# A planned attention and gated-convolution kernel: transfers paced by the megabyte, dummy products bounded by free banks, TensorE's order written out

## The chip, the cores and the metric

The kernel runs on one core of one Trainium2 chip. The metric is the time of one launch on the device, in microseconds (us). Five engines work side by side, each through its own instruction list in order: TensorE (PE, matrix products into PSUM), VectorE (DVE), ScalarE (ACT), GpSimd (POOL) and SyncE (SP), which here issues most of the transfers between HBM and SBUF. Engines meet at semaphores only.

## The reference

Batch 8, 8 heads, 576 positions, 64 elements per head. For every batch and head there are two attentions, and their sum `x` goes through a gated convolution:

```python
q_d, k_d, v_d = means of q, k, v over 4 neighbouring positions      # 144 positions
out_up = repeat(softmax(q_d k_d^T / 8) v_d, 4)                      # coarse attention
mask   = |i - j| < 4
out_local = softmax(where(mask, q k^T / 8, -1e9)) v                 # local attention
x    = (out_up + out_local) as [8, 576, 512]
gate = sigmoid(sum over k<5 of conv_w[k] * x shifted by 4-k positions)
out  = (gate * (x @ w_val)) @ w_out                                 # 512x512 weights
```

## The kernel before

**Work.** The attention runs in 16 steps `i`; a step takes four heads (two tiles `p` of 128 partitions, 32 tiles in all). On TensorE a step is `sla`, `slb` (local scores, two halves, L722), `sd` (coarse scores, L811), `odp` (coarse attention times v, L932), `xa`, `xb` (local probabilities times v, two halves, L888). `odp`, `xa` and `xb` of a step write one pair of PSUM tiles `x`; VectorE adds the coarse result in `xu` (after `xa`) and `xt` (after `xb`), both L903, and so makes a tile of `x` in SBUF.

The projections run over 10 blocks `j` of columns, 8 of 504 and 2 of 288. In a block, `v` is the product with w_val and `o` the product with w_out. Each has four output groups `c`, and in a wide block each group is four pieces `d` of three products each (`product`, L1096 to L1098: the operands are split into a high and a low part, and high times high, high times low and low times high are added). A piece is named `v2.3@0` (group 2, piece 3, block 0). Two PSUM banks of tag `v` hold the groups in turn: group `c` can begin when group `c-2` has been read, by `h` (gate times value, VectorE, L1124) for `v` and by `ob` (ScalarE, L1186) for `o`. Three double banks of tag `a` hold the attention tiles in turn.

VectorE further does for each tile the four steps `tap0` to `tap3` of the convolution (L994), for each step the row maxima and sums `mx`, `sub`, `sum`, `norm`, the transposes `turn`, `cturn`, the maxima `cmx0`, and the low parts `xl` (L969), `hlo` (L1144) and `wlo` (L1076, of the weights). The weights arrive as float64; `val` (L1049) is VectorE's integer step of their conversion. `xl`, `hlo`, `wlo` and `norm` may be put on VectorE or on GpSimd.

**What sets the order.** The program holds a planner that plays the kernel through with a table of durations (L159 to L428): every engine takes its ready operation with the earliest due time. Two engines have their own rule. TensorE takes from a list made by `tensor_order` (L473), within a window of 14; the list's head is the string `FIRST`, and from step 2 on it comes from the rates in `PACE` and `TURN`. SyncE takes transfers whose due time is within `HORIZON`, eight under way at most (L391). The instructions are then emitted in the order of the planned starts, and the semaphores follow from the order in which they were emitted: if `xu` is emitted ahead of `xb` of the same step, `xb` waits for it, because both touch the tile `x`; if it is emitted behind, it doesn't.

**Dummy products.** Before an attention group or the first piece of a projection group, the planner may set dummy products of 288 columns (`keep_warm`, L576) into the bank of that group, to keep TensorE active. Their number comes from `keep_busy` (L430), by the time since the last product.

The lines that the change touches in `keep_busy` and in the loop over the engines:

```python
gap = now - recent[-1][1]                                    # L440
begin = recent[-1][1] if recent else now - n * ns            # L446
if free[e] > now or (e == "SP" and len(flying) >= OUTSTANDING):   # L391
```

Of the kernel before, what the change touches and what calls it, by code (L numbers as in the profile page):

```python
# [162 lines left out]
class Planner:  # L163
# [102 lines left out]
    def simulate(self):  # L266
# [16 lines left out]
        head, prev, flying = 0, None, []  # L283
        code, arrived = 0, [0.0, 0.0]

        def stall(k, begin):
# [184 lines left out]


def tensor_order():  # L473
# [21 lines left out]
    whole = len(chunks) - 2 * 4 * pieces(NFULL) * 2  # L495
    marks = list(PACE) + [(NSTEP, whole - HOLD)]

    def goal(t):
        for (a, m), (b, n) in zip(marks, marks[1:]):
            if t <= b:  # L500
                return int(m + (n - m) * (t - a) / (b - a))

# [821 lines left out]
```

## Time and profile before

| | |
|---|---|
| Three runs | 367.65, 369.12, 465.03 us; median 369.12 |
| The profiled execution | 368.75 us, of which the instructions span 367.0 |
| TensorE, busy | 341.5 us (93%) |
| VectorE, busy | 309.0 us (84%) |
| ScalarE, busy | 208.3 us (57%) |
| GpSimd, busy | 158.2 us (43%) |
| Moved by DMA | 70.95 MB, mean 193 GB/s |

The profile is of one execution. Busy time of an engine is the time in which it had an instruction under way, so an engine that waits for nothing and one that runs slowly at a lowered clock both look busy. TensorE's products overlap their neighbours, so the time from one start to the next is what a product costs. A wait is put down to the engine whose semaphore came last. "Issue" is time in which an engine waited for nothing that the profile shows.

### The profile page before, as it was taken

What the parts mean: (1) busy time and instruction counts of PE and PEld (TensorE: products, weight loads), DVE (VectorE), ACT (ScalarE), POOL (GpSimd) and SP (SyncE); (2) the same over time, 40 slices, a digit from 0 to 9 for tenths busy, and PEclk for the clock granted to TensorE, in tenths of its full rate; (3) what the DMA queues carried; (4) which work ended last, traced back from release to release, by engine and by line L of the source; (5) the groups of instructions that cost most, each with busy time, mean ns of one, the idle gap of its engine ahead of it and who ended that gap; (6) DMA issues with size and microseconds to landing.
All of it is one profiled execution on the core that took longest, in us unless ns stands there. A gap on an engine that the chain in (4) does not pass through costs nothing.

```text
span 367.0 us, 12798 instructions
## 1 busy us (share of the span) xinstructions
PE 341.5 (93%) x5500; PEld 268.2 (73%) x5500; DVE 309.0 (84%) x487; ACT 208.3 (57%) x530; POOL 158.2 (43%) x170
## 2 busy tenths in 40 slices
PE   8669669699999999999999999999799999999996
PEld 5546447577787777777777777777577778788996
DVE  4699989999899999999999998999988993836720
ACT  1388556746676865587555756675376465314421
POOL 6878732955504644434453245633582323001100
PEclk9998889899999999999999999999999999999999
DMA  7999499899897799887989997969523301102012
GB/s 229 352 362 349 113 292 293 226 199 178 272 305 173 234 267 293 234 210 223 293 205 224 274 248 195 220 183 308 140 49 113 116 3 63 51 2 86 28 50 80
DMA packets 23464, 70.95 MB, mean 193 GB/s; under 512 B 3184, under 2 KB 9584, under 8 KB 23408
## 3 DMA queue, kind: packets, MB, share of 16 engines
q1 hardware_dynamic: 17504, 52.39, 41.0%
q0 software_dynamic: 5616, 17.50, 26.5%
q8 instruction: 43, 0.70, 0.7%
q10 hardware_dynamic: 288, 0.26, 0.2%
q14 instruction: 13, 0.11, 0.1%
HBM read 60.69 MB, written 9.44 MB: 191 GB/s over the span
## 4 chain that ended last, share of the span: by engine, by line
PE 62%; DVE 20%; ACT 7%; DMA 4%; issue 3%; SPq 1%; POOL 1%; ACTq 0%; POOLq 0%; DVEq 0%
PE out L1096 8%; PE val L1096 7%; PE out L1097 7%; PE out L1098 7%; DVE gp L994 7%; PE val L1098 6%; PE val L1097 6%; PE x L888 6%; PE x L932 4%; DMA qk<-in_qk 4%; PE sd L811 4%; PE sl L722 2%; DVE xt L903 2%; ACT pd L855 2%; ACT pt L574 2%
## 5 line engine op out<-in xcount | busy, mean ns | idle before, releaser
L994 DVE SCALAR_TENSOR_TENSOR gp<-xt,cw,gp 128x576 f32<-128x576 f32 x128 | 111.4, 902 | 1.3 <-ACT gp L979 0.6
L1096 PE MATMUL val<-xhs,wh_v 128*128 128x504 f32 (+1 forms) x160 | 64.0, 400 | 0.0
L1098 PE MATMUL val<-xls,wh_v 128*128 128x504 f32 (+1 forms) x160 | 60.3, 377 | 0.3 <-POOL xls L969 0.3
L1097 PE MATMUL val<-xhs,wl_v 128*128 128x504 f32 (+1 forms) x160 | 60.0, 375 | 0.0
L1096 PE MATMUL out<-hhl,wh_o 128*128 128x504 f32 (+1 forms) x144 | 58.6, 407 | 0.5 <-DVE h L1124 0.4
L1098 PE MATMUL out<-hhl,wh_o 128*128 128x504 f32 (+1 forms) x144 | 54.7, 380 | 0.0
L1097 PE MATMUL out<-hhl,wl_o 128*128 128x504 f32 (+1 forms) x144 | 54.6, 379 | 0.0
L1005 ACT ACTIVATE gp<-gp 128x576 f32<-128x576 f32 x32 | 21.9, 685 | 28.1 <-DVE gp L994 27.9
L1186 ACT ACTIVATE ob<-out 128x504 f32<-128x504 f32 (+2 forms) x40 | 21.8, 554 | 27.8 <-PE out L1098 24.0
L888 PEld LDWEIGHTS x<-pt,vw 64*64 64x64 f32 x1536 | 26.4, 138 | 14.6 <-issue 6.4
L903 DVE TENSOR_TENSOR xt<-x,od 128x288 f32<-128x288 f32 x64 | 26.0, 441 | 13.0 <-PE x L888 13.0
L1096 PEld LDWEIGHTS val<-xhs,wh_v 128*128 128x128 f32 x160 | 30.3, 190 | 8.5 <-issue 2.9
L1144 POOL TENSOR_TENSOR hhl<-h,hhl 128x504 fp32r<-128x504 f32 (+2 forms) x24 | 26.8, 1148 | 19.7 <-ACT hhl L574 19.1
L1098 PEld LDWEIGHTS val<-xls,wh_v 128*128 128x128 f32 x160 | 30.4, 190 | 5.9 <-POOL xls L969 0.7
L1096 PEld LDWEIGHTS out<-hhl,wh_o 128*128 128x128 f32 x144 | 27.0, 188 | 9.0 <-issue 3.3
L574 POOL COPY pt<-pt 32x576 f32<-32x576 f32 x23 | 16.9, 733 | 38.6 <-PE x L888 29.7
L1097 PEld LDWEIGHTS val<-xhs,wl_v 128*128 128x128 f32 x160 | 30.4, 190 | 4.1
L888 PE MATMUL x<-pt,vw 64*64 64x48 f32 x1536 | 30.1, 225 | 3.3 <-DVE xt L903 2.4
L606 POOL DMA_DIRECT2D vs<-in_vgr x21 | 20.3, 968 | 29.0 <-DMA vs<-in_vgr 20.8
L855 ACT ACTIVATE pd<-pd,crs 128x144 f32<-128x144 f32 x75 | 24.6, 405 | 12.3 <-DVE crs L849 12.2
L722 PE MATMUL sl<-qk 128*24 128x60 f32 x1536 | 26.8, 215 | 4.7 <-issue 2.0
L831 ACT ACTIVATE pd<-sd,cbi 128x144 f32<-128x144 f32 x80 | 29.9, 386 | 2.1 <-DVE h L1124 1.6
(94 smaller groups left out, 675.8 us busy)
## 6 DMA issues: line engine op xcount, KB each, us to landing
qk<-in_qk SPq DMA_DIRECT2D x64, 291.0 KB, 7.3
vw<-in_vw SPq DMA_DIRECT2D x16, 768.0 KB, 6.0
qs<-in_qkr POOLq DMA_DIRECT2D x18, 576.0 KB, 8.2
out_t<-ob SPq DMA_DIRECT2D x32, 252.0 KB, 4.6
vs<-in_vgr POOLq DMA_DIRECT2D x21, 320.0 KB, 7.5
qs<-in_qkr SPq DMA_DIRECT2D x6, 576.0 KB, 10.5
vs<-in_vgr SPq DMA_DIRECT2D x7, 320.0 KB, 7.2
raw_v<-in_w_val SPq DMA_DIRECT2D x4, 512.0 KB, 8.2
```

The source lines that it names most:

```text
L574: (nc.scalar.copy if eng is nc.scalar else eng.tensor_copy)(out=to, in_=of)
L722: nc.tensor.matmul(out=sc[32 * q : 32 * q + BQ, 2 * KW * g : 2 * KW * (g + 1)].rearrange("p (h k) -> p h k", h=2), lhsT=t[:, 1, 3 + blk : ...
L831: nc.scalar.activation(out=pd[:, g, 0:SD], in_=s["cs"][:, g], func=AF.Exp, scale=1.0 / 128.0, bias=s["bi"][:, g : g + 1], accum_out=s["csm ...
L855: nc.scalar.mul(w[:, g], w[:, g], s["crs"][:, g : g + 1])
L888: nc.tensor.matmul(out=s["x", pr][r, part, 0:HALF].rearrange("p (e g j) -> p e g j", e=2, j=BQ)[:, :, g], lhsT=s["vw"][(LO, HI)[pr], n + h ...
L903: nc.vector.tensor_tensor(out=xt, in0=s["x", pr][:, part, 0:HALF].rearrange("p (e j r) -> p e j r", e=2, r=FAC), in1=od.broadcast_to([P, 2 ...
L994: nc.vector.scalar_tensor_tensor(out=s["gp"], in0=s["xt"][:, k : k + S], scalar=cw[:, c, k : k + 1], in1=s["gp"], op0=ALU.mult, op1=ALU.add,)
L1005: nc.scalar.activation(out=s["gp"], in_=s["gp"], func=AF.Tanh, scale=0.5)
L1096: nc.tensor.matmul(out=o, lhsT=wh[:, d, col], rhs=his[d], start=d == 0, stop=False)
L1097: nc.tensor.matmul(out=o, lhsT=wl[:, d, col], rhs=his[d], start=False, stop=False)
L1098: nc.tensor.matmul(out=o, lhsT=wh[:, d, col], rhs=los[d], start=False, stop=d == NC - 1)
L1144: eng.tensor_tensor(out=t["hl"][:, cs], in0=t["h"][:, cs], in1=t["hh"][:, cs].bitcast(F32), op=ALU.subtract)
```

## The change

Five things change, all of them in the planner and its tables:

1. SyncE's transfers are paced by bytes. Counting back over the transfers that SyncE sent, the one with which 2,000,000 bytes are passed has to have landed. The planner notes it in `pace`, and `emit` adds a semaphore wait on it to the later transfer.
2. Dummy products are planned only in the time in which the bank of their group is free. 30 of them become 20; from `sd@2` on there are none.
3. TensorE's list is written out to its end in `FIRST`; `PACE`, `TURN`, `TURNS` and `HOLD` go.
4. The planner's costs of code loading change: 62 instructions at the start, 0.28 more for each operation, 2700 ns for a block instead of 5500, and on top of it the time that the bytes under way still need.
5. `SHIFT` moves 17 more due times, `HORIZON` goes from 25000 to 29000, and in `EARLY` one weight load moves ahead of one load of q and k.

By these the other engines' orders and shares change too. 14 operations come from GpSimd to VectorE: `norm` of steps 3, 9, 11 and 13, `xl` of tiles 7, 12, 17 and 25, `wlo` of chunks 1, 6 and 7, `hlo0.0@3`, `hlo2.0@5` and the half-width `hlo3.1@3`. Eight leave VectorE: to GpSimd `xl` of tiles 5 and 13, `hlo1.0@5` and four half-width `hlo3`, to ScalarE `cnorm@9`.

```diff
-    "raw4 qk6 raw5 qk7 ql6 ql7 raw6 raw7 vw2 vw3"
+    "raw4 raw5 qk6 qk7 ql6 ql7 raw6 raw7 vw2 vw3"
-HORIZON = 25000
+HORIZON = 29000
+FLIGHT = 2000000
-PACE = ((2, 10), (4, 29), (14, 189))
-HOLD = 6
-TURN = (("sla slb", 1, 3), ("sd", 1, 3), ("odp", 0, 3), ("xa", 0, 3), ("xb", 0, 4))
-    "l0 sd0 l1 sd1 odp0 x0 p2 odp1 p4 l2 p2 x1 sd2 p2"
+    "sla0 slb0 sd0 sla1 slb1 sd1 odp0 xa0 xb0 p2 odp1 p4 sla2 slb2 p2 xa1 xb1 sd2 p3 sla3 slb3 p2 sd3 p2 odp2 p2 xa2 p2 xb2 p2 sla4 p2 slb4 sd4 p3 odp3 xa3 "
...
-CODE, FETCH, BEAR = 256, 5500, 300
+CODE, FETCH, BEAR = 256, 2700, 300
...
+    def backlog(self, t):
+
+        left = sum(max(0.0, x[1]) for l in self.queue.values() for x in l) / 1e3 / self.ALONE["SP"]
+        return max(0.0, left - max(0.0, t - self.now))
...
+        def paced(now):
+
+            kept, left = [], FLIGHT
+            for x in reversed(sent):
+                left -= ops[x]["size"]
+                if left < 0:
+                    if x not in end or end[x] > now:
+                        return False
+                    kept = [x]
+                    break
+            self.behind = kept
+            return True
...
-                if free[e] > now or (e == "SP" and len(flying) >= OUTSTANDING):
+                if free[e] > now or (e == "SP" and (len(flying) >= OUTSTANDING or not paced(now))):
...
-                    begin = self.keep_busy(k, begin)
+                    begin = self.keep_busy(k, begin, banks_free(k, 0))
...
-            gap = now - recent[-1][1]
+            gap = now - max(recent[-1][1], free)
...
-            begin = recent[-1][1] if recent else now - n * ns
+            begin = max(recent[-1][1], free) if recent else now - n * ns
...
-            o["fn"](*([self.engines[self.who[k]]] if o["pick"] else []))
+            self.sent[k] = o["fn"](*([self.engines[self.who[k]]] if o["pick"] else []))
+            for x in self.pace.get(k, ()):
+                self.after(self.sent[k], self.sent[x])
...
+    def after(late, early):
+        tc.add_manual_dep(
+            late.ins,
+            early.ins.name,
+            mybir.DependencyInfo(mybir.DependencyClass.Sync, mybir.DependencyReason.DATA),
+            reason="transfers under way",
+        )
```

**TensorE around the last group of `v` in block 0.** `sl_913` are the scores of step 4, `sl_838` those of step 3; `val_2` and `val_3` are groups 2 and 3 of block 0, and `sd_912` are the coarse scores of step 3; line 579 sets the dummies. In the changed file a line stands 20 further down. Before:

```order
L722 MATMUL sl_913<-qk_78 24x60 x2
L722 MATMUL sl_913<-qk_79 24x60 x2
L579 MATMUL val_3_1000<-const-float32-1.0 128x288 [waits DVE_49]
L579 MATMUL val_3_1000<-const-float32-1.0 128x288 x4
L1096 MATMUL val_3_1000<-xhs,wh_v 128x504
L1097 MATMUL val_3_1000<-xhs,wl_v 128x504
L1098 MATMUL val_3_1000<-xls,wh_v 128x504
```

Now:

```order
L742 MATMUL sl_838<-qk_81 24x60 x2
L1116 MATMUL val_2_805<-xhs,wh_v 128x504
L1117 MATMUL val_2_805<-xhs,wl_v 128x504
L1118 MATMUL val_2_805<-xls,wh_v 128x504
L1116 MATMUL val_3_907<-xhs,wh_v 128x504 [waits DVE_49]
L1117 MATMUL val_3_907<-xhs,wl_v 128x504
L1118 MATMUL val_3_907<-xls,wh_v 128x504
L831 MATMUL sd_912<-qs_708 32x144 x20
```

The five dummies ahead of group 3 are gone, the wait for VectorE (for `h1@0`, which frees the bank) stands at the group's first product. The scores of step 4, which stood ahead of group 3, are further down the list, and the coarse scores of step 3, which stood ahead of group 2, now follow the first piece of group 3.

**VectorE around `h1@0`**, the read that frees that bank (`h_1`). `mx`, `ex<-sl` and `cmx` are row maxima and subtraction of step 3, `hhl` the low part of `h0`. Before:

```order
L1049 SCALAR_TENSOR_TENSOR raw_o_678<-raw_o_678 128x512 [waits DMAHW5_49]
L772 STREAM_TRANSPOSE pt_942<-ex 128x768
L744 TENSOR_REDUCE mx_975<-sl_749 128x24
L861 STREAM_TRANSPOSE pdt_982<-pd 128x800 [waits Activation_49]
L749 TENSOR_TENSOR ex<-sl_749,mx_975 128x24x30 [waits DVE_49]
L821 TENSOR_REDUCE cmx_988<-sd_850 128x5 [waits PE_49]
L1124 SCALAR_TENSOR_TENSOR h_1_992<-gp_593,val_1_637 128x504
L758 TENSOR_REDUCE sm_998<-ex 128x24 [waits Activation_49]
L744 TENSOR_REDUCE mx_1015<-sl_913 128x24 [waits PE_49]
L994 SCALAR_TENSOR_TENSOR gp_747<-xt_84,cw,gp_747 128x576
L994 SCALAR_TENSOR_TENSOR gp_847<-xt_85,cw,gp_847 128x576
L994 SCALAR_TENSOR_TENSOR gp_747<-xt_84,cw,gp_747 128x576 [waits DVE_49]
```

Now:

```order
L792 STREAM_TRANSPOSE pt_823<-ex 128x768 [waits Pool_49]
L881 STREAM_TRANSPOSE pdt_831<-pd 128x800 [waits Activation_49]
L1144 SCALAR_TENSOR_TENSOR h_1_836<-gp_567,val_1_643 128x504 [waits PE_49]
L1014 SCALAR_TENSOR_TENSOR gp_723<-xt_84,cw,gp_723 128x576
L1014 SCALAR_TENSOR_TENSOR gp_730<-xt_85,cw,gp_730 128x576
L1014 SCALAR_TENSOR_TENSOR gp_723<-xt_84,cw,gp_723 128x576 [waits DVE_49]
L764 TENSOR_REDUCE mx_904<-sl_838 128x24 [waits PE_49]
L769 TENSOR_TENSOR ex<-sl_838,mx_904 128x24x30 [waits DVE_49]
L1096 TENSOR_TENSOR wl_o<-raw_o_654,wh_o 128x512 [waits Activation_49]
L1096 TENSOR_TENSOR wl_o<-raw_o_640,wh_o 128x512 [waits Pool_49]
L1014 SCALAR_TENSOR_TENSOR gp_730<-xt_85,cw,gp_730 128x576
L1014 SCALAR_TENSOR_TENSOR gp_723<-xt_84,cw,gp_723 128x576
```

The three operations of step 3 (`mx`, `sub`, `cmx0`) stood ahead of `h1@0` and now stand behind it; two `wl_o` (`wlo@6`, `wlo@7`) have come in behind them from GpSimd.

**SyncE at the loads of w_val.** `DMAHW0` to `DMAHW7` are eight semaphores that SyncE's transfers use in turn. Before:

```order
L1063 DMA raw_v_253<-in_w_val 128x512 [waits DMAHW3_49]
L1063 DMA raw_v_287<-in_w_val 128x512 [waits DMAHW4_49]
L663 DMA vw_291<-in_vw 128x1536 [waits DMAHW5_49]
L601 DMA vs_295<-in_vgr 128x640 [waits DMAHW6_49]
L1063 DMA raw_v_327<-in_w_val 128x512 [waits DMAHW7_49]
L1063 DMA raw_v_331<-in_w_val 128x512 [waits DMAHW0_49]
L658 DMA qk_78<-in_qk 64x1164 [waits DMAHW1_49,DVE_49,PE_49]
L658 DMA qk_78<-in_qk 64x1164 [waits DMAHW2_49]
```

Now:

```order
L1083 DMA raw_v_285<-in_w_val 128x512 [waits DMAHW3_49]
L1083 DMA raw_v_289<-in_w_val 128x512 [waits DMAHW4_49]
L683 DMA vw_293<-in_vw 128x1536 [waits DMAHW5_49]
L621 DMA vs_326<-in_vgr 128x640 [waits DMAHW6_49,DMAHW1_49]
L1083 DMA raw_v_367<-in_w_val 128x512 [waits DMAHW7_49,DMAHW3_49]
L1083 DMA raw_v_377<-in_w_val 128x512 [waits DMAHW4_49,DMAHW0_49]
L678 DMA qk_78<-in_qk 64x1164 [waits DMAHW5_49,DVE_49,PE_49]
L678 DMA qk_78<-in_qk 64x1164 [waits DMAHW2_49]
```

Before, each transfer waits for the one that used its semaphore, eight transfers earlier. Now the third and fourth load of w_val wait for the first and second as well, and some transfers behind them wait later or earlier than by the count of eight.

## Rows read from the trace of the kernel before

**Rows 1.** The head of the profile's page.

```profile
span 367.0 us, 12798 instructions
```

**Rows 2.** Busy time by stretch, us: start and end, length, then each engine (instructions), clock.

```profile
0.00:80.00 80.00, 62.04 (x1197) 45.79 (x1197) 68.66 (x90) 45.54 (x116) 50.68 (x59) 0.91 0.87 268
80.00:280.00 200.00, 195.75 (x3446) 150.67 (x3446) 189.78 (x311) 127.25 (x336) 92.57 (x95) 1.00 0.84 224
```

**Rows 3.** Timeline of TensorE, 58 to 88 us: start, duration, engine, line, operation, idle before.

```profile
58.74 1.43 PE L811 MATMUL sd<-qs 128*32 128x144 f32 x40
...
68.58 4.38 PE L579 MATMUL val<-const-float32-1.0 128*128 128x288 f32 x10 [2.98 <-DVE h L1124]
72.58 0.61 PE L1096 MATMUL val<-xhs,wh_v 128*128 128x504 f32 x1
...
74.96 1.46 PE L932 MATMUL x<-pdt,vs 32*64 32x145 f32 x40
...
77.24 1.61 PE L888 MATMUL x<-pt,vw 64*64 64x48 f32 x96
...
79.16 0.60 PE L1096 MATMUL out<-hhl,wh_o 128*128 128x504 f32 x1
...
85.88 0.34 PE L711 MATMUL sl<-mask_b,ident_b 128*32 128x360 bf16 x4
...
86.67 0.32 PE L711 MATMUL sl<-mask_b,ident_b 128*32 128x360 bf16 x4
```

**Rows 4.** Timeline of VectorE, 44 to 77 us, same columns.

```profile
44.16 1.28 DVE L1076 TENSOR_TENSOR wl_v<-raw_v,wh_v 128x512 fp32r<-128x512 f32 x2
...
52.41 0.91 DVE L821 TENSOR_REDUCE cmx<-sd 128x5 f32<-128x720 f32 x1 [1.38 <-PE sd L811]
...
64.55 0.86 DVE L744 TENSOR_REDUCE mx<-sl 128x24 f32<-128x720 f32 x1
...
66.26 0.86 DVE L749 TENSOR_TENSOR ex<-sl,mx 128x720 f32<-128x720 f32 x1
67.05 0.89 DVE L821 TENSOR_REDUCE cmx<-sd 128x5 f32<-128x720 f32 x1
67.86 0.66 DVE L1124 SCALAR_TENSOR_TENSOR h<-gp,val 128x504 f32<-128x504 f32 x1
...
70.09 6.19 DVE L994 SCALAR_TENSOR_TENSOR gp<-xt,cw,gp 128x576 f32<-128x576 f32 x6
76.21 0.67 DVE L1144 TENSOR_TENSOR hhl<-h,hhl 128x504 fp32r<-128x504 f32 x1
```

**Rows 5.** Costliest groups of VectorE: busy us, mean ns of one.

```profile
L994 DVE SCALAR_TENSOR_TENSOR gp<-xt,cw,gp 128x576 f32<-128x576 f32 x128 | 111.4, 902 | 1.3 <-ACT gp L979 0.6
```

**Rows 6.** TensorE by stretch: length, busy, granted clock, DMA share, GB/s.

```profile
68.50:72.50 4.00, 3.92 (x9) 0.57 0.55 115
72.50:76.00 3.50, 3.50 (x44) 1.00 1.11 203
```

**Rows 7.** Who waited for whom on TensorE, 80 to 367 us: total, times, longest.

```profile
PE x L888 <- DVE xt L903: 2.4, 1, 2.4
```

**Rows 8.** Groups of VectorE that keep shapes apart: busy us, mean ns of one.

```profile
L969 DVE TENSOR_TENSOR xls<-xt,xhs 128x576 fp32r<-128x576 f32 x17 | 13.5, 810 | 2.2 <-ACT xhs L574 1.7 <-POOL xhs L574 0.5
L765 DVE TENSOR_TENSOR ex<-ex,rs 128x720 f32<-128x720 f32 x10 | 10.6, 1058 | 0.0
```

**Rows 9.** Timeline of TensorE: the longest idle time with no releaser shown.

```profile
40.26 0.71 PE L932 MATMUL x<-pdt,vs 32*64 32x145 f32 x11 [3.17 <-issue]
```

**Rows 10.** DMA issues on the page: count, KB each, us from issue to landing.

```profile
qk<-in_qk SPq DMA_DIRECT2D x64, 291.0 KB, 7.3
```

**Rows 11.** Timeline of VectorE: the integer step on the weights, two pairs apart.

```profile
38.17 4.23 DVE L1049 SCALAR_TENSOR_TENSOR raw_v<-raw_v 128x512 uint32<-128x512 uint32 x2
...
61.42 2.32 DVE L1049 SCALAR_TENSOR_TENSOR raw_o<-raw_o 128x512 uint32<-128x512 uint32 x3
```

**Rows 12.** Timeline of GpSimd at the first of those stretches.

```profile
40.16 3.46 POOL L691 TENSOR_TENSOR qs<-qs,qk 128x432 f32<-128x432 f32 x2
```

More of the change, by code (lines that the diff above doesn't have):

```diff
@@ L179, with __init__ @@
     SHARE = 0.5
-    def __init__(self, engines):
-        self.ops = {}
-        self.engines = engines
+    def __init__(self, engines, after):
+        self.ops, self.sent = {}, {}
+        self.engines, self.after = engines, after
     def op(self, key, eng, dur, fn, deps=(), free=(), banks=(), cols=(0, 0), size=0, port=(), code=0):
@@ L282, in simulate @@
         heapq.heapify(wake)
-        head, prev, flying = 0, None, []
-        code, arrived = 0, [0.0, 0.0]
+        head, prev, flying, sent, self.pace = 0, None, [], [], {}
+        code, arrived = 62, [0.0, 0.0]
         def stall(k, begin):
             o = ops[k]
-            n = o["code"] + 4 * self.idle.get(k, 0)
+            n = o["code"] + 4 * self.idle.get(k, 0) + 0.28
             dur, late, new = o["opts"]["PE"], 0.0, []
             have = arrived + new
-            for block in range(code // CODE + 1, (code + n) // CODE + 1):
+            for block in range(int(code // CODE) + 1, int((code + n) // CODE) + 1):
                 t = begin + late + dur * (block * CODE - code) / max(n, 1)
                 late += max(0.0, have[block] - t)
-                new.append(max(t, have[block]) + FETCH)
+                t = max(t, have[block])
+                new.append(t + FETCH + dma.backlog(t))
                 have = arrived + new
@@ L408, in simulate @@
                     arrived += new
-                    code += o["code"] + 4 * self.idle[k]
+                    code += o["code"] + 4 * self.idle[k] + 0.28
                     for tag, rel in o["banks"]:
@@ L420, in simulate @@
                 if o["size"]:
-                    flying += [k] * (e == "SP")
+                    if e == "SP":
+                        flying.append(k)
+                        self.pace[k] = self.behind
+                        sent.append(k)
                     dma.add("POOL" if e == "POOL" else "SP", free[e], o["size"], k)
@@ L428, in simulate, with keep_busy @@
         self.start, self.end, self.who = start, end, who
-    def keep_busy(self, k, now):
+    def keep_busy(self, k, now, free):
         dur = self.ops[k]["opts"]["PE"]
@@ L493, in some @@
         seq.extend((n, s) for n in names.split() if 0 <= s < NSTEP)
[L495 to L501, printed above, removed]
     for word in FIRST.split():
@@ L508, in tensor_order @@
             some({"l": "sla slb", "x": "xa xb"}.get(name, name), i)
-    for s in range(TURNS, NSTEP):
-        seen = 0
-        for names, ahead, n in TURN:
-            seen += n / sum(n for *_, n in TURN)
-            proj(max(0, goal(s + seen) - pos))
-            some(names, s + ahead)
     proj(len(chunks))
@@ L600, in run @@
                 u[nm] = inp.tile(shape, F32, tag=nm, name=f"{nm}{b}", bufs=2)
-                nc.sync.dma_start(out=u[nm], in_=src[b, 0])
+                return nc.sync.dma_start(out=u[nm], in_=src[b, 0])
             return run
@@ L1213, in cw_in @@
     def cw_in():
-        nc.sync.dma_start(out=cw_raw, in_=conv_w)
+        return nc.sync.dma_start(out=cw_raw, in_=conv_w)
     cw_parts = f64_parts(cw_raw)
```

16 lines of the change are left out of this document (8 added, 8 removed), and 4 rows, old and new, of the table FIRST.

## The prediction

> **What bounds the kernel now.** I read the head of the page, then busy time by stretch, then the timeline of the engine that is busiest in each stretch, and last the waits.
>
> By stretch the kernel is two kernels. From 80 to 280 us TensorE is busy 195.75 of 200 us and VectorE 189.78 [rows 2]: TensorE sets the pace, and VectorE has only 200 - 189.78 = 10.2 us to spare. From 0 to 80 us TensorE is busy 62.04 us, much of it with dummies and at a lower clock, while VectorE has 68.66 us of work [rows 2]. So the opening is a chain through VectorE's order, and what TensorE gets out of an edit there counts only as far as VectorE, or work moved behind, lets it. From the first `out` piece at 79.16 us on [rows 3] TensorE works nearly without a hole: after 80 us the one wait of size is 2.4 us of `xb` for `xu` [rows 7]. Whatever brings that first `out` piece forward, less the TensorE work that is put off beyond it, arrives at the end.
>
> **The sum starts** at the profiled execution's own 368.75 us (span 367.0 [rows 1], 1.75 around it). The median of the runs shown, 369.12, is 0.4 above it.
>
> **The dummies ahead of `v3.0@0`.** The bank comes free when `h1@0` ends; then TensorE runs ten dummy records from 68.58 and begins the real piece at 72.58 [rows 3]. All five go: 4.00 us earlier. What they bought is the clock: after 2.98 us of idle [rows 3] the granted clock was 0.57 in those 4.00 us, so mostly 1.2 GHz, and 1.00 after them [rows 6]. Left out, the pieces themselves run through that time: 4.00 x (1 - 0.57) = 1.7 us lost. In the new list the engine has the scores of step 3 and `v2.3` to do just before, so its idle time should be shorter than 2.98. I take half, 0.9, with 0 and 1.7 as ends. The Trainium skill ("TensorE: Matmul & The Clock Gate", section Why this matters for your kernels) says to avoid idle gaps between bursts of products, since the clock drops and the next burst starts slow; this speaks against leaving dummies out, and the clock of 0.57 agrees. By that rule the loss would be the whole 1.7, and on TensorE alone the gain is 0.8 us smaller.
>
> **VectorE ahead of `h1@0`.** It ended at 67.86 + 0.66 = 68.52 [rows 4]. `mx`, `sub` and `cmx0` of step 3 move behind it: 0.86 + 0.86 + 0.89 = 2.61 [rows 4]. One weight part (`wlo@1`) comes in ahead: 1.28 / 2 = 0.64 [rows 4]. So it ends at 66.55. Also `cmx0@2` waited 1.38 us for `sd@2` [rows 4], which itself stood behind two dummies that now go; the operations before it change too, so I take half, 0.7, with 0 and 1.38 as ends. `h1@0` then ends at 65.9, and `v3.0@0` begins there.
>
> **From there to the first `out` piece.** TensorE: four pieces of group 3 (three took 74.96 - 72.58 = 2.38, so 3.17), `sd@3` 1.43, `odp@2` 1.46, `xa` and `xb` 1.61 [rows 3], together 7.67, and 0.9 for the clock: 74.4. VectorE has to reach `hlo0.0@0`: six taps, `mx`, `sub`, two `wlo`, `hlo`. Taps at their mean of 902 ns [rows 5] are 5.41; with 0.86 + 0.86 + 1.28 + 0.67 [rows 4] that is 9.08, so 75.0. With the six taps as slow as they were, 6.19 [rows 4], it is 75.7. VectorE is later than TensorE: 75.4 between its two. That is 79.16 - 75.4 = 3.8 us earlier, and the clock's loss lies under VectorE's lead. Put off beyond it is `sla@4`, `slb@4`, 2 x (86.67 - 85.88) = 1.58 us [rows 3]. **Net 2.2 us.** Ends: no gain at `cmx0`, slow taps (76.4): 1.2; whole gain, taps at their mean (74.3): 3.3. The single dummies ahead of the first two `out` pieces go too; there I count nothing, because the low parts `hlo2` and `hlo3`, now on GpSimd, are what the third and fourth piece will wait for instead.
>
> **After 80 us.** Before, `xb@12` waited 2.4 us for `xu`, which VectorE reached late [rows 7]. In the new list `xb@12` no longer waits for VectorE, since `xu` is emitted behind it: 2.4 us go. But seven other `xb` still do, and `xb@9` stands just one piece behind `xa@9` where there were several. Such a wait is worth between 0 and the 2.4 seen; I take half. **Net 1.2 us.**
>
> **VectorE's load.** 14 operations come, 8 leave. Coming: four `norm` at 1.06, four `xl` at 0.81 [rows 8], two and a half `hlo` at about 0.8, three `wlo` at 0.64 [rows 4]: 11.4. Leaving: two `xl`, three `hlo` in all, one coarse `norm`: 5.0. Net 6.4 us, of which 1.9 are `wlo` in the opening, already in the sum where they stand before the first `out` piece. The rest is cost at nothing: the 10.2 us to spare cover it, and GpSimd, which loses these operations, disturbs VectorE less. Without that cover it costs up to 6.4.
>
> **Pacing, code loads, `HORIZON`.** The longest idle time of TensorE that no semaphore explains is 3.17 us, within `odp@1` [rows 9], in the stretch that VectorE bounds; under a shorter one the first `out` piece is not earlier. Transfers of 291 KB land 7.3 us after their issue [rows 10]; eight of them are 2.3 MB, so the limit of 2 MB changes little where q and k load, and more where the weights load. Cost 0, between -3.2 (the code wait goes and counts in full) and +3 (a load of the opening becomes the late one). Two returns between attention and projection fewer are within the rounding.
>
> **Sum:** 368.75 - 2.2 - 1.2 = **365.3 us**, 1.0% under the median. With the ends of its terms this case alone lies between 362 and 367.5.
>
> **Rivals.**
>
> *VectorE's stalls go as well (360.3 us).* Two integer steps on weights took 4.23 us where three later ones took 2.32, 0.77 each [rows 11]: 2.7 too much, while GpSimd ran two-input additions, 3.46 us, beside the second [rows 12]. And the six taps lost 6.19 - 5.41 = 0.8 [rows 4, 5], half of it in the sum already. If the moves of two-input work off GpSimd take such overlaps away, VectorE's chain is 2.7 + 0.4 = 3.1 us shorter, the other half of `cmx0`'s wait goes, 0.7, and of the waits after 80 us the other half, 1.2, as well: 365.3 - 5.0 = 360.3. For it: VectorE is what bounds the opening. Against: the additions beside that pair of integer steps are `qe@6`, the pooled sums of tile 6, and these stay on GpSimd. The Trainium skill ("SBUF — State Buffer", section Who interferes with whom) says that VectorE and GpSimd share one port pair as an exclusive lock, held for the whole instruction where both read SBUF with VectorE having two inputs; by that rule this rival is the outcome, and the 4.23 us agree with it.
>
> *The change brings nothing (368 us).* The eight-transfer rule already held the queue, the first pieces run at the lower clock, `out` waits for GpSimd's `hlo`, and new waits of `xb` replace the old: 368.75 less about 1.
>
> *VectorE becomes the bound: slower (372 us).* One mechanism: its net 6.4 us are not covered, since its idle time after 80 us is forced by the order (it waits for `xb`, for ScalarE's exponentials) and can't be filled. Then `xu` and `h` come late, and TensorE, whose banks they free, waits. It decides when the lock relief is under 6.4 - 10.2 x (the usable share of the idle time), which, with no relief at all, is a share under 0.63. 365.3 + 6.4 = 371.7. For it: 189.78 of 200 [rows 2]. Against: GpSimd's versions of these operations took VectorE's time as well.
>
> **Chances.** Forecast 0.50, stalls go 0.24, nothing 0.14, VectorE bound 0.12. A measurement of this kernel tells about 2% from no change: below 361.7 is faster, above 376.5 slower. Of the second case, whose own spread is some 2 us about 360.3, 0.19 lies below, and of the forecast's low side 0.05: 0.24 faster. Slower takes a third of the last case, 0.04. Within 2%: 0.72. The range reaches from 358.5 to 371.0: to the low end of the stalls case, and up to where the last case begins.
>
> **What will show it.** Right: `v3.0@0` begins within 0.2 us of the end of `h1@0`, near 66 us; the first `out` piece near 75.4; no dummies after 40 us; no wait of `xb@12`; VectorE some 315 us busy, less whatever GpSimd's relief takes off. The rival on stalls: the pair of integer steps near 2 us, first `out` piece before 73. The slower rival: TensorE busy clearly under 195 of the 200 us from 80 to 280, with waits for `xu` or `h`. The forecast is wrong if the first `out` piece stands later than 77 us, or if `xb` or the `out` pieces wait over 4 us in total after it.

## The result and the profile after

The changed kernel takes 370.64 us (median of 19 runs; the kernel before 368.47, also 19): a ratio of 1.0056, 95% interval 1.0028 to 1.0083. That is 2.1 us slower, where 365.3 was forecast. Every ratio below is against the kernel before, run in turn on the same chip. Executions more than 1.5% above the fastest of their kernel are left out of the ratios, though not of the medians.

The profiled execution took 369.84 us, 1.1 us more than that of the kernel before (368.75), so the two traces show about half of the loss. The head of its page, and busy time by stretch, as [rows 1, 2]:

```profile
span 368.1 us, 12759 instructions
```

```profile
0.00:80.00 80.00, 56.94 (x1075) 41.92 (x1075) 68.19 (x89) 44.44 (x109) 47.32 (x54) 0.89 0.88 268
80.00:280.00 200.00, 196.90 (x3545) 152.15 (x3545) 188.87 (x315) 128.88 (x348) 86.24 (x95) 0.99 0.83 224
```

From 80 to 280 us TensorE gained a little (196.90 us busy for 195.75). The loss is in the opening, where VectorE has as much work as before. The timeline of TensorE there, as [rows 3] (lines stand 20 further down: L1116 is the first product of a piece, L731 the mask of `sl`):

```profile
67.53 0.39 PE L1116 MATMUL val<-xhs,wh_v 128*128 128x504 f32 x1
...
75.89 1.78 PE L908 MATMUL x<-pt,vw 64*64 64x48 f32 x96 [1.12 <-ACT od L965]
78.64 0.64 PE L1116 MATMUL out<-hhl,wh_o 128*128 128x504 f32 x1 [0.97 <-DVE h L1144]
80.04 0.79 PE L1116 MATMUL out<-hhl,wh_o 128*128 128x504 f32 x1
...
86.03 0.34 PE L731 MATMUL sl<-mask_b,ident_b 128*32 128x360 bf16 x4
...
86.83 0.33 PE L731 MATMUL sl<-mask_b,ident_b 128*32 128x360 bf16 x4
87.71 0.49 PE L1116 MATMUL out<-hhl,wh_o 128*128 128x504 f32 x1
```

`v3.0@0` begins at 67.53 instead of 72.58, without dummies. But the first `out` piece begins at 78.64, only 0.52 earlier than before, and the first eight are done at 86.03, where they were done at 85.88. Then comes `sl@4`, 86.03 to 87.71; in the kernel before it was long done, and `sl@5` stood here [rows 3]. At `o2.0@0`, 87.7 us in both, TensorE is one pair of scores behind. VectorE in the same time, as [rows 4]:

```profile
60.58 0.67 DVE L1144 SCALAR_TENSOR_TENSOR h<-gp,val 128x504 f32<-128x504 f32 x1
...
66.01 0.63 DVE L1144 SCALAR_TENSOR_TENSOR h<-gp,val 128x504 f32<-128x504 f32 x1
66.57 3.96 DVE L1014 SCALAR_TENSOR_TENSOR gp<-xt,cw,gp 128x576 f32<-128x576 f32 x3
70.46 0.89 DVE L764 TENSOR_REDUCE mx<-sl 128x24 f32<-128x720 f32 x1
...
73.41 3.26 DVE L1014 SCALAR_TENSOR_TENSOR gp<-xt,cw,gp 128x576 f32<-128x576 f32 x3
76.60 0.67 DVE L1164 TENSOR_TENSOR hhl<-h,hhl 128x504 fp32r<-128x504 f32 x1
...
77.92 0.67 DVE L1144 SCALAR_TENSOR_TENSOR h<-gp,val 128x504 f32<-128x504 f32 x1
...
79.33 0.66 DVE L1144 SCALAR_TENSOR_TENSOR h<-gp,val 128x504 f32<-128x504 f32 x1
```

The four `h` are `h0@0` to `h3@0`. `h2@0` ends at 78.59 and lets `o0.0@0` begin; `h3@0` ends at 79.99 and `o1.0@0` follows. `h3@0`, which ended at 80.30 before, is no more than 0.3 us earlier. Where VectorE lost what the order had saved stands 30 us further up, in two places. First, its wait for `xa@0` and `xb@0` ahead of `xu0@0`, in the kernel before and in the changed one:

```profile
26.99 1.36 DVE L1049 SCALAR_TENSOR_TENSOR raw_v<-raw_v 128x512 uint32<-128x512 uint32 x1
...
29.61 0.96 DVE L772 STREAM_TRANSPOSE pt<-ex 128x768 f32<-128x768 f32 x1
...
31.27 1.55 DVE L903 TENSOR_TENSOR xt<-x,od 128x288 f32<-128x288 f32 x4 [0.62 <-PE x L888]
```

```profile
28.50 0.66 DVE L863 TENSOR_SCALAR cs<-csm 128x5 f32<-128x5 f32 x1 [0.47 <-ACT pd L851]
32.02 0.46 DVE L923 TENSOR_TENSOR xt<-x,od 128x288 f32<-128x288 f32 x1 [2.86 <-PE x L908]
...
33.18 0.97 DVE L792 STREAM_TRANSPOSE pt<-ex 128x768 f32<-128x768 f32 x1
...
39.02 1.89 DVE L1069 SCALAR_TENSOR_TENSOR raw_v<-raw_v 128x512 uint32<-128x512 uint32 x3
```

The integer step `val@1` (`raw_v`) and the transpose `turn@1` (`pt`) stood ahead of `xu0@0`; now they stand behind it, and VectorE waits 2.86 us with nothing to do. Second, the slow operations beside GpSimd have moved: three integer steps take 1.89 us now, where two took 4.23 [rows 11], but `tap1@0`, `tap0@1` and `tap2@0` take 1.9 each, beside the same `qe@6`. One of them, and GpSimd's timeline there:

```profile
43.36 1.87 DVE L1014 SCALAR_TENSOR_TENSOR gp<-xt,cw,gp 128x576 f32<-128x576 f32 x1
```

```profile
43.05 1.56 POOL L711 TENSOR_TENSOR qs<-qk 128x432 f32<-128x432 f32 x1
44.69 3.51 POOL L711 TENSOR_TENSOR qs<-qs,qk 128x432 f32<-128x432 f32 x2
```

### The profile page after: what moved, and what is told of

Same layout as the page of the kernel before. It is cut to its first block, busy times and chain, and to the rows that moved or that the text cites. A ratio compares the mean times of both kernels' runs of the same rounds, so it can differ in the third digit from the quotient of the medians.

```text
span 368.1 us, 12759 instructions
## 1 busy us (share of the span) xinstructions
PE 338.3 (92%) x5480; PEld 266.3 (72%) x5480; DVE 310.4 (84%) x493; ACT 208.9 (57%) x533; POOL 151.1 (41%) x165
## 4 chain that ended last, share of the span: by engine, by line
PE 61%; DVE 24%; DMA 8%; issue 3%; SPq 2%; ACT 1%; POOL 1%; ACTq 0%; DVEq 0%; POOLq 0%
DVE gp L1014 10%; PE out L1116 9%; PE out L1117 8%; PE out L1118 8%; PE val L1116 7%; PE val L1118 6%; PE val L1117 6%; PE x L908 5%; PE x L952 4%; PE sd L831 4%; PE sl L742 3%; DMA raw_v<-in_w_val 3%; DMA qk<-in_qk 2%; DVE h L1144 2%; DMA vw<-in_vw 2%
## 5 line engine op out<-in xcount | busy, mean ns | idle before, releaser
L1116 PE MATMUL val<-xhs,wh_v 128*128 128x504 f32 (+1 forms) x160 | 64.4, 402 | 4.6 <-DVE h L1144 4.6
L1116 PE MATMUL out<-hhl,wh_o 128*128 128x504 f32 (+1 forms) x144 | 59.1, 410 | 1.8 <-DVE h L1144 1.7
L1116 PEld LDWEIGHTS val<-xhs,wh_v 128*128 128x128 f32 x160 | 30.6, 192 | 13.8 <-DVE h L1144 5.1
L1116 PEld LDWEIGHTS out<-hhl,wh_o 128*128 128x128 f32 x144 | 27.3, 189 | 11.4 <-issue 4.1
L952 PE MATMUL x<-pdt,vs 32*64 32x145 f32 x640 | 25.6, 294 | 6.4 <-DVE pdt L881 5.3
L1118 PEld LDWEIGHTS out<-hhl,wh_o 128*128 128x128 f32 x144 | 27.5, 191 | 5.1
L875 ACT ACTIVATE pd<-pd,crs 128x144 f32<-128x144 f32 x80 | 26.2, 403 | 7.4 <-DVE crs L869 7.2
```

The source lines that it names most:

```text
L875: nc.scalar.mul(w[:, g], w[:, g], s["crs"][:, g : g + 1])
L952: nc.tensor.matmul(out=s["x", q // 2][64 * h : 64 * h + 64, 0, HALF : HALF + NG * CQ].rearrange("p (g j) -> p g j", j=CQ), lhsT=u["vs"][32 ...
L1116: nc.tensor.matmul(out=o, lhsT=wh[:, d, col], rhs=his[d], start=d == 0, stop=False)
L1118: nc.tensor.matmul(out=o, lhsT=wh[:, d, col], rhs=los[d], start=False, stop=d == NC - 1)
```

## Experiments

Theories at the start. *The chain*: VectorE's order sets when `h2@0` and `h3@0` release the banks, so dummies and TensorE's idle time ahead of them cost nothing, and `sl@4`, put off, costs its length. *The holding*: the new waits of SyncE delay loads. *The clock*: TensorE is slower for want of dummies. *The port*: GpSimd beside VectorE costs more than the planner's order can save.

Further names: `qe` are the pooled sums of q and k of a tile (VectorE or GpSimd); `rcp` and `crcp` are the reciprocals of the row sums of the local and the coarse attention, `cgrd` the step ahead of `crcp`, and `cnorm` the scaling by it (here on ScalarE); `exp`, `cbi` and `cexp0` to `cexp4` are ScalarE's exponentials and what they need; `sl` is `sla` and `slb`; `xh` is the high part of a tile of `x`, and `spr3` a copy of turned local probabilities.

In an edit `(a, b)` puts operation `a` right behind `b` on its engine; every engine otherwise keeps the planned order. `drop` leaves out the dummies ahead of an operation. But for that of e1, the edits are given in short form and not word for word. Each time is a median of 12 runs where nothing else is said.

**The holding (e1).**

```diff
-            for x in self.pace.get(k, ()):
-                self.after(self.sent[k], self.sent[x])
```

> The changed kernel, its order and dummy products untouched, but SyncE's transfers no longer held for the bytes under way. Theory of the holding (the waits delay the early loads, and that is the loss): the time falls back by 1 to 2 us, to a ratio of 0.999 to 1.002 against the kernel before. Theory of VectorE's chain (the first `out` pieces wait for h2@0 and h3@0, which come when they came before): the loads are no part of it; the ratio stays at 1.004 to 1.007, and the first `out` product stays at 78.6 us within 0.4.

Measured: 369.95 us, 1.0034 (1.0012 to 1.0055), between the two expectations; the first `out` product at 78.98, so the opening's end does not move. The time is 0.8 us below that of the change, with intervals that overlap: whether the holding is a part of the loss stays open.

**The dummies of `v3.0@0` alone (e2), in the kernel before.**

```diff
+drop ("v3.0", 0)
```

> The kernel before, with the five dummies ahead of v3.0@0 left out and nothing else: the 4.00 us that the prediction counted as the delay, alone. The prediction's step (TensorE is the one that is late here): v3.0@0 begins at 68.5 us, and 2 to 4 us of it come out of the time, a ratio of 0.989 to 0.995. Theory of VectorE's chain: v3.0@0 begins at 68.5 us all the same, but the first `out` product can't begin before h2@0 ends at 78.2 us, nor o1.0@0 before h3@0 ends at 80.3; 0.1 to 0.5 us, a ratio of 0.9985 to 1.000. Theory of the clock (the dummies keep TensorE at its upper level for what follows): products between 72 and 86 us run at 1.2 GHz, and the time rises by 0.5 to 1.5 us.

Measured: 368.62 us, 1.0006 (0.9978 to 1.0035). The trace: `h1@0`, then `v3.0@0` at once, then what waits next, on VectorE and TensorE:

```profile
69.43 0.66 DVE L1124 SCALAR_TENSOR_TENSOR h<-gp,val 128x504 f32<-128x504 f32 x1
78.63 0.67 DVE L1124 SCALAR_TENSOR_TENSOR h<-gp,val 128x504 f32<-128x504 f32 x1
```

```profile
70.14 0.50 PE L1096 MATMUL val<-xhs,wh_v 128*128 128x504 f32 x1 [3.32 <-DVE h L1124]
79.45 0.72 PE L579 MATMUL out<-const-float32-1.0 128*128 128x288 f32 x2 [1.63 <-DVE h L1124]
```

TensorE reaches the first `out` piece early and waits 1.63 us for `h2@0`. The 4.00 us of my first step were worth nothing that the times show (the interval allows 0.8 us at most), as the chain says.

**`sl@4` put back (e3), and the read of the first `out` bank ahead (e5), in the changed kernel.** To stand ahead of `odp@2`, `sl@4` needs a bank that only the exponentials of `sd@3` free, so these move too.

```diff
+(cmx0@3, sub@3) (cbi@3, exp@3) (cexp0..4@3, behind cbi@3)
+(sla@4, sd@3) (slb@4, sla@4) (odp@2, v3.3@0)
+(ob0@0, xh@5)       # e5 only
```

> The changed kernel with sl@4 issued after sd@3, some 17 us earlier, as in the kernel before, and what that needs: cmx0@3 and the exponentials of sd@3 ahead of it on VectorE and ScalarE, odp@2 after v3.3@0. Theory of VectorE's chain: h3@0 comes when it came (80.0 us), and the 1.58 us of sl@4 move from behind the first eight `out` pieces into TensorE's idle time ahead of them: 1.0 to 1.6 us less than the changed kernel, a ratio of 1.001 to 1.003 against the kernel before. If the loss lies elsewhere (in the other 280 us, or in the loads): the ratio stays at 1.004 to 1.007.

> The changed kernel with sl@4 early as in the run e3_scores4_early, and ob0@0 (the read of the first `out` bank) ahead of cnorm@3 on ScalarE. Theory now: TensorE can't begin o2.0@0 before ScalarE has read the bank of o0.0@0, near 87.7 us in the kernel before, in the changed one and in e3; sl@4 moved away from there left 1.61 us of idle time in its place. With the read ahead of cnorm@3, o2.0@0 begins at once behind o1.3@0, near 86.2 us; 1.0 to 1.6 us less than e3, a ratio of 0.999 to 1.001. If the scores have nothing to do with the loss, or cturn@3 (later by 0.5 us) makes odp@3 wait for as much: the ratio stays at 1.003 to 1.005.

Measured: e3 370.09 us, 1.0043 (1.0015 to 1.0070): a miss. Its TensorE timeline shows where the 1.58 us went:

```profile
87.76 0.49 PE L1151 MATMUL out<-hhl,wh_o 128*128 128x504 f32 x1 [1.61 <-ACT ob L1241]
```

`o2.0@0` waits for ScalarE to read the bank of `o0.0@0`, behind `cnorm@3`; in the changed kernel `sl@4` filled just this wait. With the read moved ahead (e5), `o2.0@0` begins at 85.90: 368.59 us, 0.9997 (0.9974 to 1.0020), as expected.

```profile
85.90 0.50 PE L1152 MATMUL out<-hhl,wh_o 128*128 128x504 f32 x1
```

The read alone, with `sl@4` left late (e12):

> The changed kernel with the read of the first `out` bank (ob0@0) ahead of cnorm@3 on ScalarE, and sl@4 left where the change put it. If sl@4 fills TensorE's wait for that read, as in the changed kernel's trace, the read comes earlier for nothing: 1.004 to 1.007. If the order on ScalarE was the whole of what e5_scores4_early_ob0 gave back: 0.999 to 1.001.

Measured: 369.34 us, 1.0018 (0.9989 to 1.0047), between the two expectations. In its trace `o2.0@0` still follows `sl@4`, so I have no mechanism for a gain, and how e5's gain divides between the two edits stays open. The control, on the chip of e14 to e16:

> The changed kernel as it is, on one chip with the next three: 1.003 to 1.008 against the kernel before. If it comes out at 1.000 to 1.002, the loss hangs on the chip, and e12_changed_ob0 (1.0018) changed nothing.

Measured: 370.10 us, 1.0056 (1.0023 to 1.0088). The loss is there again on this chip. In this execution VectorE waited 4.01 us at `xu0@0`:

```profile
33.06 0.46 DVE L923 TENSOR_TENSOR xt<-x,od 128x288 f32<-128x288 f32 x1 [4.01 <-PE x L908]
```

**The chain shortened, in the kernel before (e4, e7).**

```diff
+(sum@3, h3@0) (rcp@3, sum@3) (mx@4, rcp@3)   drop ("v3.0", 0)   # e4
+(qe@4, crcp@1)                                                 # e7
```

> The kernel before without the five dummies ahead of v3.0@0, and with sum@3, mx@4 and rcp@3 (1.85 us of VectorE) moved from ahead of h3@0 to right behind it. Theory of VectorE's chain: h2@0 and h3@0 come 1.6 to 1.9 us earlier, the first `out` product with them, near 76.8 us; 1.3 to 2.0 us less, a ratio of 0.9945 to 0.9965. If TensorE's dummies alone were the bound, the ratio is that of the kernel without the dummies alone. If what is put off is missed at once (step 3's probabilities, sl@5): waits of xa@3 or odp@3 behind 88 us take back 1 us or more, a ratio of 0.998 to 1.002.

> The kernel before with one operation moved: qe@4 (1.94 us on VectorE) from behind xt1@0 to ahead of xu0@0, where VectorE waits for xa@0 (0.62 us in the profiled run of the kernel before, 1.25 and 2.19 in those of the runs without the dummies of v3.0@0, whose orders are the same up to there). Theory of VectorE's chain: the wait is filled, h0@0 to h3@0 come 0.6 to 1.6 us earlier, TensorE follows through the dummies of v3.0@0, and the whole time falls by as much, a ratio of 0.9955 to 0.9985. If TensorE or the loads set the opening's end: 0.999 to 1.001.

Measured: e4 368.53 us, 0.9989 (0.9964 to 1.0015), a miss: VectorE's time from `xu0@0` to the end of `h3@0` was 48.0 us, 0.5 less than in e2 and not 1.85, since the six taps took 7.00 us; and `cgrd@3`, later now, delayed `cnorm@3` and the read behind it, so `o2.0@0` came at 89.70, after 0.74 us of waiting. e7 367.71 us, 0.9974 (0.9950 to 0.9997): the wait at `xu0@0` filled is worth 1 us even where it was short. Its profiled execution, the slowest of the twelve (369.75 us), does not show how: the wait is gone, but `h3@0` ends at 80.8, after two `wlo` beside GpSimd's `qe@6` had taken 3.54 us.

**The port (e8), in the kernel before.**

```diff
+self.who["qe", 6] = "DVE"   (qe@6, qe@5)
```

> The kernel before with qe@6 on VectorE, behind qe@5, instead of on GpSimd. Theory of the shared port: val@2, val@3 and tap0@0 took 2.47, 1.83 and 1.92 us beside GpSimd's qe@6, and take 0.69, 0.69 and 0.81 without it, 4.0 us less for 1.87 more on VectorE: the chain is 1.5 to 2.2 us shorter, a ratio of 0.994 to 0.9965. If the slow operations follow the next thing on GpSimd (xl@2, the casts) instead: VectorE pays 1.9 us and gets less than that back, 0.999 to 1.005.

Measured: 365.47 us (10 runs), 0.9908 (0.9876 to 0.9941), more than expected. The operations that stood beside `qe@6`, on VectorE:

```profile
36.55 3.77 DVE L715 TENSOR_REDUCE qs<-qk 128x432 f32<-128x1728 f32 x2
...
41.05 1.29 DVE L1076 SCALAR_TENSOR_TENSOR raw_v<-raw_v 128x512 uint32<-128x512 uint32 x2
42.25 0.81 DVE L1021 SCALAR_TENSOR_TENSOR gp<-xt,cw,gp 128x576 f32<-128x576 f32 x1
```

1.29 us for the pair that took 4.23 [rows 11], 0.81 for a tap that took 1.92. VectorE does 1.9 us more work, and from `xu0@0` to the end of `h3@0` it needs 45.7 us instead of 49.0. The Trainium skill ("SBUF — State Buffer", section Who interferes with whom) calls the port that the two engines share an exclusive lock. The trace agrees so far: with `qe@6` gone from GpSimd the three operations take 2.10 us instead of 6.15; whether the port is locked or shared no run here shows.

**Both (e9), and the chain again (e16).** e9 is e7 and e8; e16 is e9 with the moves of e4 and `(ob0@0, spr3@3)`.

> The kernel before with both moves: qe@6 on VectorE behind qe@5, and qe@4 ahead of xu0@0. Theory of VectorE's chain: the two gains (3.4 us and 1.0 us where each was made alone) are of one chain and add up, h3@0 ends near 76.5 us, and the ratio is 0.986 to 0.990. If another bound comes up first (sd@2, for which cmx0@2 waited 0.94 and 1.99 us in those runs): no more than the move of qe@6 alone, 0.990 to 0.993.

> The kernel before with qe@6 on VectorE and qe@4 ahead of xu0@0 (e9_qe4_qe6, ratio 0.984), and also sum@3, rcp@3 and mx@4 behind h3@0 and ob0@0 ahead of cnorm@3 on ScalarE. Theory of VectorE's chain, with the way over cnorm@3 as the reason for the miss of e4: h3@0 ends 1.6 to 1.9 us earlier than in e9, near 72.8 us, o2.0@0 follows o1.3@0 and sl@5 at once, and the ratio is 0.978 to 0.982. If step 3's probabilities are missed in any case (odp@3 waits for cturn@3): no gain on e9, 0.983 to 0.988.

Measured: e9 363.68 us (6 runs), **0.9839** (0.9788 to 0.9890), the fastest of all. `h3@0` ends at 74.5, 5.8 us earlier than before, and TensorE follows: `o2.0@0` begins at 81.79 instead of 87.67. VectorE, and that piece:

```profile
29.70 1.90 DVE L716 TENSOR_REDUCE qs<-qk 128x432 f32<-128x1728 f32 x1
31.86 1.55 DVE L931 TENSOR_TENSOR xt<-x,od 128x288 f32<-128x288 f32 x4 [0.25 <-PE x L916]
...
38.75 1.29 DVE L1077 SCALAR_TENSOR_TENSOR raw_v<-raw_v 128x512 uint32<-128x512 uint32 x2
...
73.88 0.66 DVE L1152 SCALAR_TENSOR_TENSOR h<-gp,val 128x504 f32<-128x504 f32 x1
```

```profile
81.79 0.49 PE L1124 MATMUL out<-hhl,wh_o 128*128 128x504 f32 x1
```

e16 365.52 us, 0.9932 (0.9900 to 0.9963): slower than e9, and outside both expectations. `h3@0` comes only 0.3 us earlier, and `odp@3` waits for `cturn@3` and then on nothing that the profile shows:

```profile
84.29 1.45 PE L964 MATMUL x<-pdt,vs 32*64 32x145 f32 x36 [0.86 <-DVE pdt L893]
87.18 0.46 PE L964 MATMUL x<-pdt,vs 32*64 32x145 f32 x4 [1.44 <-issue]
```

Step 3's softmax, put off behind `h3@0`, is missed at once.

**The changed kernel without its early dummies (e6), and with `qe@6` on VectorE (e10; e11 with the moves of e5 as well).**

```diff
+drop ("xa", 0), ("sla", 2)                     # e6
+self.who["qe", 6] = "DVE"   (qe@6, qe@5)       # e10, e11
```

> The changed kernel without the two dummies ahead of xa@0 and the four ahead of sla@2. Theory of the early dummies: xu0@0 on VectorE waits for xa@0, which stands behind 2.2 us of dummies; without them xu0@0 begins near 30 us instead of 32.0, the whole of VectorE's chain to h3@0 moves up by 1.3 to 2.0 us, and the ratio falls to 0.998 to 1.001. Theory of the clock: TensorE is then at 1.2 GHz for longer (xa@0 and xb@0 1.5 us each, sla@2 to v0.0@0 up to 2 us more), and half or more of it is lost again: 1.002 to 1.005. If the loads set the chain at 35 us (qk of pair 2): no change, 1.003 to 1.006.

> The changed kernel with qe@6 on VectorE behind qe@5. Theory of the shared port: the change only moved GpSimd's qe@6 from beside val@2, val@3 and tap0@0 to beside tap1@0, tap0@1 and tap2@0 (1.87, 1.87 and 1.86 us for 0.81 each), so that it costs 3.2 us less 1.9 here: h3@0 comes 1.3 to 2.0 us earlier, a ratio of 0.999 to 1.002. If the changed kernel's VectorE is not what sets the end of the opening: 1.004 to 1.007.

> The changed kernel with qe@6 on VectorE and with sl@4 early and the read of the first `out` bank ahead of cnorm@3, as in e5_scores4_early_ob0. If the two losses are separate (VectorE's chain, and TensorE's work that can't be done ahead of the pieces): their sum, 2.5 to 4 us less than the changed kernel, a ratio of 0.994 to 0.998. If the second was only a way around the first: no better than the better of the two alone, 0.998 to 1.002.

Measured: e6 368.19 us, 0.9945 (0.9901 to 0.9988), but the ratio is from seven of the twelve executions, and the profiled one, 373.98 us, is not among them. There `xu0@0` began at 30.78, as expected, and yet `h3@0` ended at 81.0. It settles nothing. e10 370.81 us, 1.0061 (1.0031 to 1.0091), and e11 368.33, 0.9997 (0.9966 to 1.0028): here `qe@6` on VectorE brings nothing, a miss for the port alone.

**Dummies put back into TensorE's waits (e14; e15 with `qe@6` on VectorE).** In the profiled execution of e10 the granted clock of 78 to 90 us was 0.74, and the first eight `out` pieces took 8.5 us (6.4 in that of the control).

```diff
+self.idle["odp", 2], self.idle["xa", 2] = 3, 2
```

> The changed kernel with three dummies ahead of odp@2 and two ahead of xa@2, where TensorE waits 1.2 and 1.3 us, and 1.05 us more ahead of the first `out` product. Theory of the clock (the dummies that the change dropped around 66 to 81 us kept the level for the first `out` pieces): the granted clock of 78 to 90 us rises from 0.86 to 0.95 or more, the first eight pieces take 5.6 to 6.1 us from the first product instead of 7.4, and 0.5 to 1.3 us come out of the time, a ratio of 1.001 to 1.004. If TensorE's clock there follows something else: the dummies cost up to 0.5 us, 1.004 to 1.008.

> The same dummies, and qe@6 on VectorE. Theory of the clock: now the 1.4 us by which VectorE's chain is shorter come out as well, 0.996 to 1.001. If the changed kernel gains nothing from qe@6 for another reason (TensorE's work put off, the read of the first `out` bank): as e14_changed_dummies or e10_changed_qe6, 1.003 to 1.007.

Measured: e14 370.89 us, 1.0083 (1.0050 to 1.0117); e15 371.75, 1.0059 (1.0017 to 1.0100; from eight of twelve executions). Busy time of 78 to 90 us in the changed kernel, in the control, in e10 and in e14 (the last three columns: clock, DMA share, GB/s):

```profile
78.00:90.00 12.00, 11.36 (x141) 8.48 (x141) 10.19 (x18) 9.64 (x27) 9.07 (x10) 0.86 0.77 168
```

```profile
78.00:90.00 12.00, 10.57 (x195) 8.23 (x186) 11.21 (x20) 9.46 (x27) 8.78 (x10) 1.00 0.75 186
```

```profile
78.00:90.00 12.00, 11.96 (x136) 9.29 (x137) 9.05 (x16) 8.93 (x26) 9.09 (x10) 0.74 0.81 174
```

```profile
78.00:90.00 12.00, 11.56 (x241) 9.06 (x242) 11.21 (x20) 9.86 (x27) 9.12 (x10) 1.00 0.79 172
```

The clock is at its upper level in e14, and the time is no better than the control's. But the control is at that level too, without the dummies: the clock differs here between two executions of one order, so e14 does not test it. Where it was lower it cost time: the first eight pieces took 7.4 us at 0.86 and 8.5 at 0.74, for 6.4 in the control and in e14. The control is at 1.00 and as slow as the changed kernel (369.62 and 369.84 us), so the clock is not the whole loss; its part in the executions that were not profiled stays open.

In e15's execution a wait takes back what `qe@6` gave. VectorE:

```profile
40.19 1.94 DVE L735 TENSOR_REDUCE qs<-qk 128x432 f32<-128x1728 f32 x1
42.05 1.89 DVE L1096 SCALAR_TENSOR_TENSOR raw_v<-raw_v 128x512 uint32<-128x512 uint32 x3
...
50.67 1.55 DVE L950 TENSOR_TENSOR xt<-x,od 128x288 f32<-128x288 f32 x4 [2.02 <-PE x L935]
```

In the changed order `val@1` stands behind `qe@5`, and now behind `qe@6` as well. ScalarE's high part, `v0.1@0` and `xa@1` wait for it, and `xu0@1` for them: 2.02 us of idle time take back what the port gave. In the kernel before `val@1` is done at 28.3 us. In e10's execution there is no such wait: `h3@0` ends at 79.4, 1.8 us earlier than in the control, and the eight pieces, at 0.74, take 2.1 us longer. So the gain goes in two ways in two executions, and why `qe@6` brings nothing in the median stays open.

**The wait at `xu0@0` filled (e17), and `sl@4` early as well (e18), in the changed kernel.**

```diff
+(crcp@1, cgrd@1) (turn@1, crcp@1) (qe@4, turn@1)       # e17; e18 adds those of e5
```

> The changed kernel with crcp@1, turn@1 and qe@4 (2.9 us of VectorE) moved ahead of xu0@0, into the wait for xa@0; nothing else. Theory now: the change left this wait empty, since it put val@1 behind it; filled, everything on VectorE behind it up to h3@0 comes 2 to 3 us earlier, h3@0 near 78 us (80.0 and 81.2 in the two profiled runs of the changed kernel), and the ratio falls from 1.0056 to 0.997 to 1.001. If v0.1@0 and xa@1 on TensorE hold VectorE up again, as in e15_changed_qe6_dummies: a new wait at xu0@1 of 1 us or more, and 1.002 to 1.006.

> The same, with sl@4 early and the read of the first `out` bank ahead of cnorm@3 as in e5_scores4_early_ob0 (0.9997). If the two losses are separate: their gains add up, 0.991 to 0.996, below the kernel before. If both only move the same end of the opening: 0.997 to 1.001.

Measured: e17 367.72 us, 0.9971 (0.9938 to 1.0004): three operations moved ahead of one wait bring 3 us against the changed kernel. e18 364.52 (6 runs), 0.9890 (0.9846 to 0.9934): the gains add. e17's VectorE:

```profile
29.00 0.94 DVE L820 STREAM_TRANSPOSE pt<-ex 128x768 f32<-128x768 f32 x1
31.64 1.95 DVE L736 TENSOR_REDUCE qs<-qk 128x432 f32<-128x1728 f32 x1 [1.70 <-DMA qk<-in_qk]
33.51 1.54 DVE L951 TENSOR_TENSOR xt<-x,od 128x288 f32<-128x288 f32 x4
...
37.72 1.60 DVE L1097 SCALAR_TENSOR_TENSOR raw_v<-raw_v 128x512 uint32<-128x512 uint32 x1
...
76.89 0.67 DVE L1172 SCALAR_TENSOR_TENSOR h<-gp,val 128x504 f32<-128x504 f32 x1
```

`h3@0` ends at 77.6 (80.0 and 81.2 in the two profiled executions of the changed kernel). In this execution VectorE now waits for a load at this place, 1.70 us. Of the 2.4 us by which `h3@0` comes earlier than in the first of the two, 1.3 are there at the integer steps (37.72 for 39.02); the rest lies behind them, where two operations instead of three are slow beside `qe@6`. And `qe@4` stood behind `xu0@0` in the kernel before as well, where moving it brought 1 us (e7). So e17 fills the wait further than the old order did, and its 3 us are not the size of what the wait cost.

## Why the prediction was wrong

The failed step is "From there to the first `out` piece", and the start of the one ahead of it.

1. *Dummies of `v3.0@0`, 4.00 us.* They went, and `v3.0@0` began 5 us earlier. Alone that is worth nothing that the times show (e2). I had said that a TensorE edit in the opening counts only as far as VectorE lets it; the sum then set VectorE's time in its place, and that time was wrong, as follows.
2. *VectorE ahead of `h1@0`, end at 65.9.* It ended at 66.64. The three operations did move, and `cmx0@2` no longer waited (1.38 us, of which I had counted 0.7), but I added up from 44 us on, with the time up to there as it was. `h0@0` ended at 61.25, 1.25 us later than before, because VectorE idles ahead of `xu0@0`. I had compared VectorE's order at `h1@0` alone and not up there, and counted nothing for `val@1` and `turn@1`, which had filled the wait. e17 fills the wait and brings 3 us, though in part by other ways. And `v3.0@0` did not follow `h1@0` at once: it began at 67.53, behind `v2.3`, since group 2 had waited 4.62 us for `h0@0`.
3. *`hlo0.0@0` at 75.0 to 75.7, first `out` piece at 75.4.* It ended at 77.27. The six taps took 7.22 us instead of 5.41 to 6.19 [rows 4, 5]: two of GpSimd's two-input operations run beside them (`wlo`, 1.59 us from 66.86, and an `hlo`, 1.82 us from 74.24), where one did (1.60 us from 72.60). This fits e8, but no run tests these two. And the first piece did not wait for it: two banks hold the groups in turn, so it waits for `h2@0`, which the kernel's description says and my sum left out. 3.8 us were forecast, 0.52 came, and the first eight pieces gave up 0.67, more than all of it: the granted clock of 78 to 90 us was 0.86, and 1.00 before. The sign that I had named for a wrong forecast, a first `out` piece later than 77 us, came true.
4. *`sl@4` put off, 1.58 us.* The size was right. But it is the price of a lead that did not come, so it is a loss in full (e5, as far as e12 leaves it).
5. *After 80 us, 1.2 us.* `xb@12` waits no more, as forecast. From the end of the eight pieces to the end of the span it is 281.1 us before, and 282.1 less the 1.6 of `sl@4` after: 0.6 us of gain. New are 1.4 us within `slb@13`, which nothing shown releases, and 0.8 at `odp@7`, for VectorE; as [rows 7]:

```profile
PE sl L742 <- issue: 1.4, 1, 1.4
PE x L952 <- DVE pdt L881: 0.8, 1, 0.8
```

6. *VectorE's load and the holding, 0.* Right for the load: VectorE is busy 310.4 us (309.0 before), with no new bound behind 80 us. For the holding e1 leaves open whether it cost part of the loss.

The 370.64 us lie inside the stated range, at its upper end; that is owed to the width of the range and not to the sum. The low end that I gave the forecast's own case, 362, is a slip: 368.75 - 3.3 - 2.4 is 363.0. Of the rivals, "VectorE becomes the bound" (372) was nearest in time, but by luck: its mechanism did not occur, since TensorE is busy 196.90 of the 200 us from 80 to 280 and waits 0.7 us for `h` after the opening. "Brings nothing" (368) was nearest in mechanism, and counted no loss for `sl@4`. The rival on stalls had a sound mechanism, worth 3.4 us (e8), and the right objection, that `qe@6` stays on GpSimd.

## What to carry to other kernels

Where an engine's order is a chain, add it up from its start, and look at each of its waits: what stood there, and does it still? Ahead of a piece name every release it needs, its bank's too, before you count a gain at the latest operand. When work is put off to bring something forward, first show that it comes forward; if not, the work put off is the loss.

## What the runs showed of the hardware

- GpSimd's `qe@6` (4.9 us of GpSimd) cost VectorE 4.0 us in three operations in the kernel before; done on VectorE it costs 1.9 (e8).
- Idle time of TensorE that nothing shown releases turns up elsewhere in each order: 3.17 us in `odp@1` [rows 9] before, 1.41 in `slb@13` after, 3.52 in `slb@5` in e6.
- One order of instructions gave waits of 2.86 and 4.01 us at the same place in two executions: the granted clock of `xa@0` and `xb@0` was 0.71 in the first and 0.50 in the second. In the same two, the clock of 78 to 90 us was 0.86 and 1.00, and eight pieces took 7.4 and 6.4 us. A single profile of an opening is good to about 1 us here: `h3@0` ended at 80.0 and 81.2.
